# Linear attention and a gated layer on one core: where the output projection accumulates, and when the bonus, state and r steps are issued

## The chip, the cores and the metric

The kernel runs on one NeuronCore of a Trainium2 chip. The metric is device time in microseconds (us) of one execution. Before the change three runs gave 119.29, 119.60 and 119.94 us, median 119.6.

## What is computed

Batch 4, 8 heads, 768 steps, head size 48, so 384 columns for each step. The first half is a recurrence with a 48x48 state for each head, the second a causal convolution over five steps that gates a projection:

```python
for t in range(S):
    cur = np.einsum('bhd,bhe->bhde', u[None] * kt, vt)
    y[:, :, t] = np.einsum('bhd,bhde->bhe', rt, state + cur)
    state = w[None, :, :, None] * state + np.einsum('bhd,bhe->bhde', kt, vt)
...
gate_pre += conv_w[k][None, None, :] * xp[:, k:k + S, :]   # k = 0..4
gate = 1.0 / (1.0 + np.exp(-gate_pre))
val = x @ w_val
return (gate * val @ w_out)
```

## The kernel before

The recurrence is computed in chunks of 128 steps. Two chunks make a unit of 256 steps, so a batch has 3 units and there are N = 12 units. The loop at the end (L551) runs iterations i = 0 to 12, as a software pipeline of two stages: iteration i does the attention side of unit i and the output side of unit f = i - 1. Nothing reorders the instructions afterwards: each engine executes them as the loop writes them, and semaphore waits are put in where tiles depend on each other.

Steps of an iteration, in the order in which TensorE (PE) gets them:

- `y_out(f)` (L390): 80 small matmuls in two PSUM banks, one for each chunk. ScalarE (ACT) copies each bank to `xT` (L428).
- `attn(i)` (L324): scores of the two chunks, each in its own two-bank tile `at_ps` of a pool with two such tiles. VectorE (DVE) multiplies each with the causal mask (`mask_at`, L343).
- `conv(f)` (L431): 40 matmuls, then two sigmoids on ACT (`gate`, L453).
- `bonus(i)` (L298): 8 tiny matmuls into columns 384 to 399 of the one `kv_ps` bank; DVE copies them out to `s_sb` (L314), which stands on DVE behind the two masks. GpSimd (POOL) multiplies v with it (`dv`, L317).
- `transp_r` (L243): transposes of one head pair of a later batch's r, which POOL (in the start-up DVE) has scaled into a ring of four buffers `rs` (L236). They go to the single `tr_ps` bank and are copied to `rT` (L250).
- `value(f)` (L456): x times w_val into two PSUM banks; DVE multiplies each with its gate into `hT` (L480).
- `state(i, 0)` (L350), into columns 0 to 383 of the same `kv_ps` bank that held the bonus, and on DVE `decay` (L379), which writes `z` (L385).
- `transp_k(i+1)` (L270) into `tr_ps`; ACT copies it to `kT` (L280); DVE makes `pr` of it (L291).
- `project(f)` (L485): for each of the two chunks three matmuls with 384 columns, into a bank of the pool `ps_mm`, and an ACT copy to `o_sb` (L499). The pool `ps_mm` has two banks, which `y_out`, `conv`, `value` and `project` take in turn.
- `state(i, 1)`, which the last unit of a batch lacks, and in some iterations a second `transp_r`.

The table `r_plan` (L539) says in which iterations the head pairs of batches 1, 2 and 3 are scaled and transposed. SyncE (SP) issues all loads in program order, k and v three iterations ahead. The weight w_out is loaded by three DMAs (L195 to L197), 768 KB, since the last of the three row tiles is kept a second time with its halves exchanged; one ACT cast makes `wout` of it (L229).

Of the kernel before, what the change touches and what calls it, by code (L numbers as in the profile page):

```python
# [8 lines left out]
F32 = mybir.dt.float32  # L9
# [7 lines left out]
def kernel(  # L17
# [169 lines left out]


    wv_st = consts.tile([128, NT, DM], F32)
    wo_st = consts.tile([128, 4, DM], F32)  # L190

    def load_weights():
        nc.sync.dma_start(out=wv_st, in_=moe_w_val.rearrange("(t p) n -> p t n", p=128))
        wo = moe_w_out.rearrange("(t p) n -> p t n", p=128)
        nc.sync.dma_start(out=wo_st[:, 0::2, :], in_=wo[:, 0::2, :])  # L195
        nc.sync.dma_start(out=wo_st[64:128, 1::2, :], in_=wo[0:64, 1:3, :])
        nc.sync.dma_start(out=wo_st[0:64, 1::2, :], in_=wo[64:128, 1:3, :])  # L197

    wval = consts.tile([128, NT, 4, 128], BF16)
    wout = consts.tile([128, 4, DM], BF16)  # L200
# [23 lines left out]
    def cast_weights():  # L224
        wv = wv_st.rearrange("p k (t x) -> p k t x", x=128)
        nc.gpsimd.tensor_copy(wval[:, :, 0::2, :], wv[:, :, 0::2, :])
        nc.gpsimd.tensor_copy(wval[:, :, 1::2, 64:128], wv[:, :, 1:3, 0:64])
        nc.gpsimd.tensor_copy(wval[:, :, 1::2, 0:64], wv[:, :, 1:3, 64:128])
        nc.scalar.copy(out=wout, in_=wo_st)  # L229


    st = {}
# [1 line left out]
    def scale_r(b, p, eng):  # L234
        hs = slice(2 * p, 2 * p + 2)
        eng.tensor_tensor(  # L236
            out=rs_t[p][:, :, :, 0:D].rearrange("p j a d -> p a j d"),
            in0=r_st[b][:, hs, :].rearrange("p a (j d) -> p a j d", d=D),
            in1=dr[:, hs],
            op=ALU.mult,  # L240
        )

    def transp_r(b, p, dve=False, pool=None):  # L243
        if p == 0:
            st["rT", b] = wk.tile([128, NP, S], BF16, name="rT", bufs=3)
        pool, name = (ps_mm, "mm_ps") if pool else (ps_tr, "tr_ps")
        tr = pool.tile([128, J, 128], BF16, name=name)
        for j in range(J):
            nc.tensor.transpose(tr[:, j, :], rs_t[p][:, j].rearrange("p a x -> p (a x)"), ident)  # L249
        (nc.vector.tensor_copy if dve else nc.scalar.copy)(  # L250
            out=st["rT", b][:, p, :].rearrange("x (p j) -> x p j", j=J),
            in_=tr.rearrange("x j p -> x p j"),
        )
# [231 lines left out]
    def project(n):  # L485
        b, cu = divmod(n, NU)
        hT = st["hT", n]
        o_sb = outp.tile([128, U, DM], F32, name="o_sb")
        for cl in range(U):
            o_ps = ps_mm.tile([128, DM], F32, name="mm_ps")  # L490
            for j, (i, c0) in enumerate(((0, cl * C), (1, cl * C), (cl, W))):
                nc.tensor.matmul(  # L492
                    out=o_ps,
                    lhsT=hT[:, i, c0 : c0 + C],
                    rhs=wout[:, 2 + cl if j == 2 else i, :],
                    start=(j == 0),
                    stop=(j == 2),
                )
            nc.scalar.copy(out=o_sb[:, cl, :], in_=o_ps)  # L499
# [11 lines left out]
    def ok(n):  # L511
        return 0 <= n < N

    load_weights()
    load_kv(1, "v")
    load_kv(2, "k")
    prep_conv()
    spin(80)
# [11 lines left out]
    for par in range(2):  # L530
# [5 lines left out]
        nc.gpsimd.tensor_copy(wcm[rows, :, par, :], wct[rows, :, None].to_broadcast([64, NP, D]))  # L536


    r_plan = {  # L539
        1: (1, (0, 1)),  # L540
        2: (1, (2, 3)),
        3: (2, (0, 1)),
        4: (2, (2,)),
        5: (2, (3,)),
        6: (3, (0, 1)),
        7: (3, (2,)),
        8: (3, (3,)),
    }
    r_load = {0: 1, 2: 2, 4: 3}

    for i in range(N + 1):  # L551
        f = i - 1
        if i == 0:
            load_kv(2, "v")
        if i in r_load:
            load_r(r_load[i])
        if ok(i + 3):
            load_kv(i + 3, "kv")
        rb, rp = r_plan.get(i, (0, ()))
        if ok(f):  # L560
            y_out(f)
        if ok(i + 1):
            cast_v(i + 1)
        for p in rp[:1]:
            scale_r(rb, p, nc.gpsimd)
        if ok(i + 1):
            scale_k(i + 1, nc.gpsimd)
        for p in rp[1:]:
            scale_r(rb, p, nc.gpsimd)
        if ok(i):  # L570
            for cl in range(U):
                attn(i, cl)
                mask_at(i, cl)
        if ok(f):
            conv(f)
        if ok(i):
            bonus(i)
            bonus_v(i)
        if rp:
            transp_r(rb, rp[0])  # L580
# [9 lines left out]
        ends = i % NU == NU - 1  # L590
        for p in rp[1:] if ends else ():
            transp_r(rb, p)
        if ok(i + 1):
# [7 lines left out]
        for p in () if ends else rp[1:]:  # L601
            transp_r(rb, p)
# [1 line left out]
_INS = ['r', 'k', 'v', 'w', 'u', 'moe_w_val', 'moe_conv_w', 'moe_w_out']  # L604
_OUTS = [((4, 768, 384), 'float32')]
# [25 lines left out]
```

## Time and profile before

| | |
|---|---|
| median of three runs | 119.6 us |
| the profiled execution's own time | 118.9 us |
| its span, first to last instruction | 116.4 us |
| mean granted TensorE clock | 0.932 |
| busy share of the span: PE, DVE, ACT, POOL | 82%, 59%, 62%, 55% |
| `y_out` starts of iterations 3, 4, 7, 8, 9 in the trace | 43.19, 50.75, 72.80, 79.59, 86.54 us |

A row of the timeline has the start in us, the duration, the engine, the line, the operation, the tiles, and in brackets how long the engine sat idle before and what ended that. Durations of PE rows contain the latency of the last matmul, so that the next row starts before the row ends. In a row of the waits stand who waited for whom, the sum in us, the number of times and the longest. A row of the windows gives for each engine the busy time in that stretch, then the granted clock (PEclk).

### The profile page before, as it was taken

To read this page: it belongs to the slowest core of one execution; us is meant where nothing else is said; L and a number is where in the kernel's file an instruction comes from. 1 tells how busy PE (TensorE), PEld (TensorE's weight loads), DVE (VectorE), ACT (ScalarE), POOL (GpSimd) and SP (SyncE) were. 2 spreads that over 40 slices of the span, in tenths; PEclk is the share of its full clock that TensorE was granted. 3 is DMA by queue.
4 is the path that set the end of the run, shared out by engine and by line. 5 is a ranking of instruction groups with operands and counts; after the bars stand their busy time and mean duration, and the time that the engine had idled before them with its cause. 6 is when DMAs were issued, how large, how long until landed. Compare 5 with 4: busy or idle time off the path is not lost.

```text
span 116.4 us, 5181 instructions
## 1 busy us (share of the span) xinstructions
PE 95.0 (82%) x2285; PEld 78.4 (67%) x2285; DVE 68.7 (59%) x110; ACT 72.5 (62%) x130; POOL 64.5 (55%) x71
## 2 busy tenths in 40 slices
PE   5999536763989779989979898999988998989660
PEld 5699425553858658769768685887967787785520
DVE  5397594073454925749739297484956779493030
ACT  4396970782268767787656886868768474834430
POOL 7963448207998578781935969469280825013000
PEclk9999965685599999999999999999999999999996
DMA  1999999999899989799979888892873030110303
GB/s 27 298 241 199 260 269 183 203 247 276 172 202 220 340 206 260 161 246 271 299 156 245 179 206 170 219 194 76 187 156 143 0 135 6 68 72 6 141 0 135
DMA packets 58578, 20.60 MB, mean 177 GB/s; under 512 B 50486, under 2 KB 58556, under 8 KB 58556
## 3 DMA queue, kind: packets, MB, share of 16 engines
q1 hardware_dynamic: 58428, 20.26, 71.9%
q8 instruction: 18, 0.29, 1.1%
q0 software_dynamic: 128, 0.00, 0.1%
q14 instruction: 4, 0.03, 0.1%
HBM read 15.54 MB, written 4.72 MB: 174 GB/s over the span
## 4 chain that ended last, share of the span: by engine, by line
PE 56%; SPq 17%; ACT 10%; DMA 5%; issue 4%; DVE 4%; POOL 1%; ACTq 0%; DVEq 0%; POOLq 0%
PE mm_ps L400 12%; SPq L72 12%; PE mm_ps L444 10%; PE mm_ps L463 8%; PE mm_ps L492 5%; PE at_ps L331 5%; DMA r_st<-in_r_dram 5%; PE tr_ps L249 4%; PE tr_ps L277 4%; ACT o_sb L499 4%; ACT kT L280 4%; PE mm_ps L472 3%; DVE pr L291 2%; DVE hT L480 2%; PE kv_ps L305 2%
## 5 line engine op out<-in xcount | busy, mean ns | idle before, releaser
L343 DVE TENSOR_TENSOR at<-at_ps,mask 128x1024 bf16<-128x1024 f32 x24 | 28.2, 1219 | 13.2 <-PE at_ps L331 13.2
L317 POOL TENSOR_TENSOR dv<-v_st,s_sb 128x768 bf16<-128x768 f32 x12 | 17.7, 1475 | 29.4 <-DVE s_sb L314 28.1
L256 POOL TENSOR_TENSOR ks<-k_st,dk 128x768 bf16<-128x768 f32 x11 | 20.0, 1819 | 1.6 <-DMA k_st<-in_k_dram 1.6
L236 POOL TENSOR_TENSOR rs<-r_st,dr 128x576 bf16<-128x576 f32 x12 | 16.8, 1402 | 6.9 <-DMA r_st<-in_r_dram 6.9
L280 ACT COPY kT<-tr_ps 128x1024 bf16<-128x1024 bf16 x11 | 11.1, 1011 | 12.3 <-PE tr_ps L277 12.3
L480 DVE TENSOR_TENSOR hT<-mm_ps,gate 128x384 bf16<-128x384 f32 x24 | 12.7, 557 | 9.7 <-PE mm_ps L472 8.4
L291 DVE TENSOR_TENSOR pr<-tr_ps,rT 128x1024 bf16<-128x1024 bf16 x11 | 7.6, 692 | 13.0 <-ACT kT L280 13.0
L492 PE MATMUL mm_ps<-wout,hT 128*128 128x384 bf16 x72 | 14.4, 327 | 0.5 <-DVE hT L480 0.5
L453 ACT ACTIVATE gate<-mm_ps 128x384 bf16<-128x384 f32 x24 | 10.5, 488 | 6.5 <-PE mm_ps L444 6.4
L428 ACT CAST xT<-mm_ps 128x384 bf16<-128x384 f32 x24 | 11.2, 480 | 4.1 <-PE mm_ps L400 3.4
L463 PE MATMUL mm_ps<-xT,wval 128*128 128x256 bf16 x72 | 12.5, 284 | 1.5 <-ACT gate L453 1.5
L250 ACT COPY rT<-tr_ps 128x768 bf16<-128x768 bf16 x13 | 10.5, 805 | 4.6 <-PE tr_ps L249 4.6
L444 PE MATMUL mm_ps<-xT,cwd 64*64 64x256 bf16 (+1 forms) x480 | 12.5, 247 | 1.0 <-ACT xT L428 0.6
L499 ACT COPY o_sb<-mm_ps 128x384 f32<-128x384 f32 x24 | 10.6, 490 | 4.2 <-PE mm_ps L492 4.2
L265 ACT CAST vb<-v_st 128x768 bf16<-128x768 f32 x12 | 10.0, 835 | 4.6 <-DMA v_st<-in_v_dram 4.6
L444 PEld LDWEIGHTS <-cwd 64*64 64x64 bf16 x480 | 11.5, 107 | 1.9 <-issue 0.5
L385 DVE TENSOR_TENSOR z<-kv_ps,wcm 128x384 bf16<-128x384 f32 x20 | 11.0, 549 | 1.6 <-PE kv_ps L369 0.9
L331 PE MATMUL at_ps<-rT,kT 48*128 48x128 bf16 x192 | 7.6, 217 | 3.4 <-ACT kT L280 2.8
L400 PE MATMUL mm_ps<-at,vb 128*32 128x128 bf16 x384 | 10.2, 226 | 0.1
L492 PEld LDWEIGHTS <-hT 128*128 128x128 bf16 x72 | 6.4, 98 | 4.8 <-DVE hT L480 2.0
L249 PE MATMUL tr_ps<-ident,rs 128*128 128x128 bf16 x78 | 6.8, 225 | 3.4 <-POOL rs L236 1.9
L127 PE MATMUL mm_ps<-ident 128*128 128x128 bf16 x96 | 8.3, 268 | 1.4 <-POOL ident masks.py:199 1.4
(74 smaller groups left out, 156.9 us busy)
## 6 DMA issues: line engine op xcount, KB each, us to landing
k_st<-in_k_dram SPq DMA_DIRECT2D x24, 192.0 KB, 4.7
v_st<-in_v_dram SPq DMA_DIRECT2D x24, 192.0 KB, 4.0
out_dram<-o_sb SPq DMA_DIRECT2D x11, 384.0 KB, 3.4
r_st<-in_r_dram SPq DMA_DIRECT2D x6, 576.0 KB, 5.5
r_st<-in_r_dram SPq DMA_DIRECT2D x4, 288.0 KB, 4.0
wv_st<-in_moe_w_val_dram SPq DMA_DIRECT2D x1, 576.0 KB, 5.1
wo_st<-in_moe_w_out_dram SPq DMA_DIRECT2D x1, 384.0 KB, 6.2
wo_st<-in_moe_w_out_dram SPq DMA_DIRECT2D x2, 192.0 KB, 5.5
```

Source lines behind the costliest of these rows:

```text
L72: nc.sync.dma_start(out=d[n][:, cl], in_=src[b, :, t0 : t0 + C, :].transpose([1, 0, 2]))
L236: eng.tensor_tensor(out=rs_t[p][:, :, :, 0:D].rearrange("p j a d -> p a j d"), in0=r_st[b][:, hs, :].rearrange("p a (j d) -> p a j d", d=D ...
L256: eng.tensor_tensor(out=ks_t[n % 3][:, :, :, :, 0:D].rearrange("p c n a d -> p c (n a) d"), in0=k_st[n], in1=dk[:, None, :, :].to_broadcas ...
L280: nc.scalar.copy(out=st["kT", n].rearrange("x n (c i) -> x c n i", c=U), in_=tr)
L317: nc.gpsimd.tensor_tensor(out=dv_t[n % 2].rearrange("p c (h d) -> p (c h) d", d=D), in0=v_st[n].rearrange("p c h d -> p (c h) d"), in1=st[ ...
L343: nc.vector.tensor_tensor(out=st["at", n, cl].rearrange("p a n i -> p (a n) i"), in0=st["at_ps", n, cl].rearrange("p a n i -> p (a n) i"), ...
L400: nc.tensor.matmul(out=y_ps[32 * q : 32 * q + 32, T, :], lhsT=lt, rhs=rh, start=q not in first, stop=last, skip_group_check=True,)
L444: nc.tensor.matmul(out=g_ps[i][64 * qo : 64 * qo + 64, o0 : o0 + n0], lhsT=cwd[rows, T, t, :], rhs=xT[rows, T, t0 + c0 + t : t0 + c0 + t + ...
L463: nc.tensor.matmul(out=v_ps[:, 0:W], lhsT=wval[:, kt, i, :], rhs=xT[:, kt, t0 : t0 + W], start=(kt == 0), stop=(kt == NT - 1), skip_group_ ...
L480: nc.vector.tensor_tensor(out=hT[:, i], in0=v_ps, in1=st["gate", n][:, i], op=ALU.mult)
L492: nc.tensor.matmul(out=o_ps, lhsT=hT[:, i, c0 : c0 + C], rhs=wout[:, 2 + cl if j == 2 else i, :], start=(j == 0), stop=(j == 2),)
L499: nc.scalar.copy(out=o_sb[:, cl, :], in_=o_ps)
```

## The change

Five edits:

1. `project` accumulates in a tile of the score pool `ps_at`, both chunks in one tile of two banks, in place of two banks of `ps_mm`. Its matmuls are put so that the first two of chunk 0 need only the first half of `hT`.
2. `state(i, 0)` is issued directly behind `bonus`, ahead of `transp_r` and `value`. Its `decay` stays behind `value`, except in iteration 0.
3. r of batch 1 (the second batch): nothing of it is transposed in iteration 1 any more. Pairs 0 and 1 are scaled on POOL at the end of iteration 1, pair 2 on POOL and pair 3 on DVE in iteration 2, and all four transposes stand in iteration 2, pairs 1 and 3 copied by DVE; `transp_k(3)` and `prod(3)` come behind them. In the other iterations the second transpose always follows `state(i, 1)`.
4. w_out is loaded once, by one DMA of 576 KB; three ACT casts make `wout` of it. The v of unit 1 is loaded ahead of the weights.
5. v of unit 1 is cast behind the weight casts.

```diff
+    wo_st = consts.tile([128, NT, DM], F32)
...
-        nc.sync.dma_start(out=wo_st[:, 0::2, :], in_=wo[:, 0::2, :])
-        nc.sync.dma_start(out=wo_st[64:128, 1::2, :], in_=wo[0:64, 1:3, :])
-        nc.sync.dma_start(out=wo_st[0:64, 1::2, :], in_=wo[64:128, 1:3, :])
+        nc.sync.dma_start(out=wo_st, in_=moe_w_out.rearrange("(t p) n -> p t n", p=128))
...
-        nc.scalar.copy(out=wout, in_=wo_st)
+        nc.scalar.copy(out=wout[:, 0::2, :], in_=wo_st[:, 0::2, :])
+        nc.scalar.copy(out=wout[64:128, 1::2, :], in_=wo_st[0:64, 1:3, :])
+        nc.scalar.copy(out=wout[0:64, 1::2, :], in_=wo_st[64:128, 1:3, :])
...
+        oo_ps = ps_at.tile([128, 2, NP, 128], F32, name="at_ps")
         for cl in range(U):
-            o_ps = ps_mm.tile([128, DM], F32, name="mm_ps")
-            for j, (i, c0) in enumerate(((0, cl * C), (1, cl * C), (cl, W))):
+            o_ps = oo_ps[:, cl].rearrange("p n x -> p (n x)")[:, 0:DM]
+            parts = [(0, cl * C, 0), (1, cl * C, 1)]
+            parts.insert(1 + cl, (cl, W, 2 + cl))
+            for j, (i, c0, k) in enumerate(parts):
...
-                    rhs=wout[:, 2 + cl if j == 2 else i, :],
+                    rhs=wout[:, k, :],
...
+    load_kv(1, "v")
     load_weights()
-    load_kv(1, "v")
...
-        2: (1, (2, 3)),
+        2: (1, (), (2,), (), (0, 1, 2, 3)),
...
         if ok(i):
             bonus(i)
             bonus_v(i)
-        if rp:
-            transp_r(rb, rp[0])
-        if ok(f):
-            value(f)
-        if ok(i):
             state(i, 0)
-            decay(i, 0)
+        for p in r2:
+            scale_r(rb, p, nc.gpsimd)
+        if i == 2:
+            scale_r(rb, 3, nc.vector)
         if i == 0:
+            decay(0, 0)
             state(0, 1)
             decay(0, 1)
             cast_weights()
...
+            cast_v(1)
+        if rt:
+            transp_r(rb, rt[0])
+        if ok(f):
+            value(f)
+        if ok(i) and i > 0:
+            decay(i, 0)
+        if i == 2:
+            transp_r(rb, 1, dve=True)
+        elif ok(i + 1):
             transp_k(i + 1)
             prod(i + 1)
         if ok(f):
             project(f)
+        if i == 2:
+            transp_r(rb, 2)
         if ok(i) and i > 0:
             state(i, 1)
             decay(i, 1)
+        if i == 2:
+            transp_r(rb, 3, dve=True)
+            transp_k(i + 1)
+            prod(i + 1)
+        else:
+            for p in rt[1:]:
+                transp_r(rb, p)
```

Three places show what the built programs make of it. `Activation_49`, `DVE_49`, `PE_49` and `Pool_49` are the semaphores of ACT, DVE, PE and POOL; the lines of the changed kernel stand some lower or higher than those of the one before.

The first is PE in iteration 9, behind the convolution. Before, the last bonus matmul (L305) is followed by the value matmuls (L463, L472) and these by the state matmuls (L360):

```order
L305 MATMUL kv_ps<-uw_205,pr 128x2
L463 LDWEIGHTS wval
L463 MATMUL mm_ps<-xT_190,wval 128x256 [waits Activation_49]
...
L472 MATMUL mm_ps<-xT_190,wval 128x128
L360 LDWEIGHTS ks_177
L360 MATMUL kv_ps<-vb_185,ks_177 128x96 [waits DVE_49]
```

In the changed kernel (bonus L304, state L359, value L462):

```order
L304 MATMUL kv_ps<-uw_205,pr 128x2
L359 LDWEIGHTS ks_177
L359 MATMUL kv_ps<-vb_185,ks_177 128x96 [waits DVE_49]
...
L462 LDWEIGHTS wval
L462 MATMUL mm_ps<-xT_190,wval 128x256 [waits Activation_49]
```

The state matmuls have moved ahead of the value matmuls with their wait on DVE. The value waited for there is that of the copy to `s_sb`, in both kernels.

The second is PE at the projection of iteration 8 and the start of `y_out` behind it, before (L492, L400):

```order
L492 LDWEIGHTS hT [waits DVE_49]
L492 MATMUL mm_ps<-wout,hT 128x384 [waits PE_49]
L492 LDWEIGHTS hT [waits DVE_49]
...
L492 MATMUL mm_ps<-wout,hT 128x384 [waits PE_49]
L492 LDWEIGHTS hT
...
L400 MATMUL mm_ps<-rT,z 32x128 [waits Activation_49]
```

And in the changed kernel (L494, L399), where the second wait for `hT` stands before the third matmul:

```order
L494 LDWEIGHTS hT [waits DVE_49]
L494 MATMUL at_ps<-wout,hT 128x384
L494 LDWEIGHTS hT [waits DVE_49]
...
L494 MATMUL at_ps<-wout,hT 128x384 [waits Activation_49]
L494 LDWEIGHTS hT
...
L399 MATMUL mm_ps<-rT,z 32x128 [waits PE_49]
```

The wait for ACT has moved from the first matmul of `y_out` to the fourth matmul of the projection, the first of chunk 1. The value waited for is that of the first copy to `o_sb` of the same projection: both chunks write one tile now. On ACT that copy stands behind the copy to `kT`, as before.

The third is PE at the end of iteration 2 in the changed kernel, where r of batch 1 is transposed (L248) around the projection and ahead of `transp_k` (L276):

```order
L248 MATMUL tr_ps<-ident,rs_181 128x128 [waits Activation_49]
...
L494 LDWEIGHTS hT [waits DVE_49]
...
L248 MATMUL tr_ps<-ident,rs_182 128x128 [waits DVE_49]
...
L248 MATMUL tr_ps<-ident,rs_183 128x128 [waits Activation_49]
...
L276 MATMUL tr_ps<-ident,ks_177 128x128 [waits DVE_49]
```

Each of the four waits for the copy of the step before it out of the one `tr_ps` bank, by ACT and DVE in turn. Before, one such transpose stood at the end of iteration 1 and two in iteration 2, of which only the last stood directly ahead of `transp_k`.

More of the change, by code (lines that the diff above doesn't have):

```diff
@@ L189 @@
     wv_st = consts.tile([128, NT, DM], F32)
-    wo_st = consts.tile([128, 4, DM], F32)
+    wo_st = consts.tile([128, NT, DM], F32)
     def load_weights():
         nc.sync.dma_start(out=wv_st, in_=moe_w_val.rearrange("(t p) n -> p t n", p=128))
-        wo = moe_w_out.rearrange("(t p) n -> p t n", p=128)
-        nc.sync.dma_start(out=wo_st[:, 0::2, :], in_=wo[:, 0::2, :])
-        nc.sync.dma_start(out=wo_st[64:128, 1::2, :], in_=wo[0:64, 1:3, :])
-        nc.sync.dma_start(out=wo_st[0:64, 1::2, :], in_=wo[64:128, 1:3, :])
+        nc.sync.dma_start(out=wo_st, in_=moe_w_out.rearrange("(t p) n -> p t n", p=128))
     wval = consts.tile([128, NT, 4, 128], BF16)
@@ L539 @@
     r_plan = {
-        1: (1, (0, 1)),
-        2: (1, (2, 3)),
[L542 to L547, printed above, removed]
+        1: (1, (), (), (0, 1), ()),
+        2: (1, (), (2,), (), (0, 1, 2, 3)),
+        3: (2, (0,), (1,), (), (0, 1)),
+        4: (2, (2,), (), (), (2,)),
+        5: (2, (3,), (), (), (3,)),
+        6: (3, (0,), (1,), (), (0, 1)),
+        7: (3, (2,), (), (), (2,)),
+        8: (3, (3,), (), (), (3,)),
     }
@@ L558 @@
             load_kv(i + 3, "kv")
-        rb, rp = r_plan.get(i, (0, ()))
+        rb, r0, r1, r2, rt = r_plan.get(i, (0, (), (), (), ()))
         if ok(f):
             y_out(f)
-        if ok(i + 1):
+        if ok(i + 1) and i > 0:
             cast_v(i + 1)
-        for p in rp[:1]:
+        for p in r0:
             scale_r(rb, p, nc.gpsimd)
@@ L567 @@
             scale_k(i + 1, nc.gpsimd)
-        for p in rp[1:]:
+        for p in r1:
             scale_r(rb, p, nc.gpsimd)
@@ L589 @@
             cast_weights()
[L590 to L593, printed above, removed]
+            cast_v(1)
[8 more added lines that the diff above has]
+        elif ok(i + 1):
             transp_k(i + 1)
@@ L600 @@
             decay(i, 1)
-        for p in () if ends else rp[1:]:
-            transp_r(rb, p)
+        if i == 2:
[5 more added lines that the diff above has]
+                transp_r(rb, p)
 _INS = ['r', 'k', 'v', 'w', 'u', 'moe_w_val', 'moe_conv_w', 'moe_w_out']
```

## Prediction

> **What bounds the kernel now.** I read the page first, then who waited for whom, then the timeline of single iterations, and last the granted clock by windows.
>
> ```profile
> span 116.4 us, 5181 instructions
> PE 95.0 (82%) x2285; PEld 78.4 (67%) x2285; DVE 68.7 (59%) x110; ACT 72.5 (62%) x130; POOL 64.5 (55%) x71
> ```
>
> PE is the fullest engine, and what counts is when it stands still. The waits:
>
> ```profile
> PE mm_ps L400 <- ACT o_sb L499: 2.4, 6, 0.6
> PE kv_ps L360 <- DVE s_sb L314: 2.0, 1, 2.0
> PE tr_ps L249 <- POOL rs L236: 1.9, 1, 1.9
> PE mm_ps L463 <- ACT gate L453: 1.5, 4, 0.6
> ```
>
> The first, third and fourth are what this change touches: `y_out` waiting for the output copies, r of batch 1 arriving late, `value` waiting for the gates. The second tells most. In iteration 0, the only one in which the state matmuls follow the bonus at once, they waited 2.0 us for the copy to `s_sb` and started 0.06 us after its end:
>
> ```profile
> 17.67 0.16 DVE L314 COPY s_sb<-kv_ps 128x16 f32<-128x16 f32 x1
> 17.89 0.50 PE L360 MATMUL kv_ps<-vb,ks 128*128 128x96 bf16 x4 [1.97 <-DVE s_sb L314]
> ```
>
> Iteration 8 shows where that copy stands otherwise:
>
> ```profile
> 81.27 2.35 DVE L343 TENSOR_TENSOR at<-at_ps,mask 128x1024 bf16<-128x1024 f32 x2 [0.92 <-PE at_ps L331]
> 82.42 0.35 PE L305 MATMUL kv_ps<-uw,pr 128*128 128x2 bf16 x8
> 82.64 0.49 PE L249 MATMUL tr_ps<-ident,rs 128*128 128x128 bf16 x6
> 83.54 0.16 DVE L314 COPY s_sb<-kv_ps 128x16 f32<-128x16 f32 x1
> 84.39 0.61 PE L277 MATMUL tr_ps<-ident,ks 128*128 128x128 bf16 x8
> 84.84 1.14 PE L492 MATMUL mm_ps<-wout,hT 128*128 128x384 bf16 x6
> 85.09 1.01 ACT L280 COPY kT<-tr_ps 128x1024 bf16<-128x1024 bf16 x1 [1.00 <-PE tr_ps L277]
> 86.00 0.87 ACT L499 COPY o_sb<-mm_ps 128x384 f32<-128x384 f32 x2
> 86.54 0.35 PE L400 MATMUL mm_ps<-rT,z 128*32 128x128 bf16 x12 [0.56 <-ACT o_sb L499]
> ```
>
> DVE spends 81.27 to 83.54 on the two masks, so `s_sb` ends at 83.70, while PE is through with the bonus at 82.64. PE fills that gap with transposes and `value`. Likewise the first output copy on ACT starts at 86.00, behind `kT`, long after its three matmuls; PE has used that time for the second three.
>
> **The state matmuls behind the bonus.** PE takes its instructions in order, and behind the state matmuls stand `transp_r`, `value`, `transp_k` and the projection. The state can start 0.06 us after `s_sb`, here at 83.76. PE then idles from 82.64 to 83.76, 1.12 us, where it idled nowhere. The work moved does not change in length. Iterations 3 to 7 differ from this by 0.1 at most: six times 1.12, 6.7 us. In iterations 9 to 11 there is no r left, and part of the wait was there already:
>
> ```profile
> 89.37 0.35 PE L305 MATMUL kv_ps<-uw,pr 128*128 128x2 bf16 x8
> 90.02 0.49 PE L463 MATMUL mm_ps<-xT,wval 128*128 128x256 bf16 x3 [0.29 <-ACT gate L453]
> 90.48 0.17 DVE L314 COPY s_sb<-kv_ps 128x16 f32<-128x16 f32 x1
> ```
>
> The first instruction behind the bonus starts at 90.02 now, and would start at 90.71 (90.48 + 0.17 + 0.06): 0.69 us more, in 9 and in 10. In 11 the state's 0.33 us lay beside the wait for `hT`; ahead of `value` it lies on the path, so 1.0. That is 2.4, and 9.1 us in all. The bounds are 0.1 us either way for each of the nine.
>
> **The projection in the score banks.** The wait of `y_out` for the copies goes. But the fourth matmul now waits for the first copy, and that copy is queued behind `kT`. From the start of `transp_k` at 84.39 the first copy ends at 86.49 and releases PE at 86.54: 2.15 us. What started at that moment was `y_out`; now it is the second three matmuls, 0.50 us (half of 0.99), and `y_out` comes behind them. So 0.5 us are added, not saved. Where `state(i, 1)` follows, it stood in the shadow of the wait and no longer does; iteration 7:
>
> ```profile
> 77.45 0.61 PE L277 MATMUL tr_ps<-ident,ks 128*128 128x128 bf16 x8
> 78.87 0.33 PE L360 MATMUL kv_ps<-vb,ks 128*128 128x96 bf16 x4
> 79.59 0.35 PE L400 MATMUL mm_ps<-rT,z 128*32 128x128 bf16 x12 [0.23 <-ACT o_sb L499]
> ```
>
> Again 2.14 from `transp_k` to `y_out`; now 2.15 + 0.50 + 0.33 = 2.98, so 0.83 more, in 4, 7, 9 and 10: 3.3 us. In 3 and 6 a transpose follows that waited for `pr` anyway, so 0.5 there as in 5 and 8: 2.0 us. The last two projections have no `kT` ahead of them; the last of all:
>
> ```profile
> 110.01 0.49 PE L463 MATMUL mm_ps<-xT,wval 128*128 128x256 bf16 x3 [0.58 <-ACT gate L453]
> 110.77 1.05 DVE L480 TENSOR_TENSOR hT<-mm_ps,gate 128x384 bf16<-128x384 f32 x2 [4.90 <-PE mm_ps L472]
> 112.42 0.96 ACT L499 COPY o_sb<-mm_ps 128x384 f32<-128x384 f32 x2 [2.08 <-PE mm_ps L492]
> ```
>
> The new order runs one matmul more before the second half of `hT`: 0.16 us gained. Then the first copy must end (0.54 from its start), three matmuls run (0.33 to the start of the third and 0.38 from there to the copy), and the second copy starts at 1.25 where it started at 0.48 (half of 0.96). Net 0.6 us in 12; in 11, where `y_out` follows, 0.50 - 0.16 = 0.35. Together 6.3 us.
>
> **Weights, v and r at the start.** Iteration 1:
>
> ```profile
> 27.00 0.16 DVE L314 COPY s_sb<-kv_ps 128x16 f32<-128x16 f32 x1
> 28.36 0.82 PE L249 MATMUL tr_ps<-ident,rs 128*128 128x128 bf16 x6 [1.90 <-POOL rs L236]
> 28.97 0.85 PE L463 MATMUL mm_ps<-xT,wval 128*128 128x256 bf16 x3
> 31.53 1.02 PE L277 MATMUL tr_ps<-ident,ks 128*128 128x128 bf16 x8
> 34.86 0.35 PE L400 MATMUL mm_ps<-rT,z 128*32 128x128 bf16 x12
> ```
>
> The clock stood at half from 28.98 to 32.39:
>
> ```profile
> 28.98:32.39 3.41, 3.41 (x28) 2.87 (x27) 1.67 (x3) 0.80 (x1) 3.41 (x3) 0.50 0.91 177
> ```
>
> Without r the state starts at 27.22, behind `s_sb`; state and value take 2.56 (28.97 to 31.53). `transp_k` would start at 29.8 at half clock, or 29.4 if the clock is up by 29. From there 2.98 to `y_out` at full clock gives 32.4, not 34.86: a gain of 2.4 us; if the clock stays low until 32.4, 33.4, a gain of 1.5. I take 2.4, since PE then stands still little after 27.2. That w_out is loaded once saves 192 KB of loads ahead of r; its three casts on ACT stand ahead of `kT` of unit 1 and take up to 0.8 us longer than the one did. I set both at nothing against each other, with 0.7 us either way.
>
> In iteration 2 the four transposes come together:
>
> ```profile
> L250 ACT COPY rT<-tr_ps 128x768 bf16<-128x768 bf16 x13 | 10.5, 805 | 4.6 <-PE tr_ps L249 4.6
> L250 DVE COPY rT<-mm_ps 128x768 bf16<-128x768 bf16 x1 | 1.0, 957 | 0.7 <-PE mm_ps L249 0.7
> 38.80 0.16 DVE L314 COPY s_sb<-kv_ps 128x16 f32<-128x16 f32 x1
> 43.19 0.35 PE L400 MATMUL mm_ps<-rT,z 128*32 128x128 bf16 x12 [0.56 <-ACT o_sb L499]
> ```
>
> From `y_out` (34.86) the state starts at 4.16 (38.80 + 0.22); state, first transpose and value take 1.75 as in iteration 8 (82.64 to 84.39), so 5.91; the second transposes end at 6.34. Their copy on DVE stands behind `hT` and `z` and ends at about 8.2, the projection as well. Third transposes to 8.65; ACT, busy with the second output copy until 8.85, copies to 9.65; fourth from 9.7, copied on DVE from 10.2 to 11.2; `transp_k` to 11.7, and `y_out`. It took 8.33 (34.86 to 43.19): 3.4 us more. At least 2.4, if the copies start a quarter of a microsecond earlier each.
>
> **The clock.** Cut into stretches of 3.41 us, the granted clock is whole or half in each:
>
> ```profile
> 11.93:15.34 3.41, 1.88 (x35) 1.40 (x32) 1.82 (x3) 3.41 (x5) 1.81 (x3) 1.00 0.98 289
> 15.34:18.75 3.41, 0.98 (x16) 0.66 (x13) 2.75 (x5) 1.45 (x2) 1.50 (x2) 0.50 1.15 212
> 107.50:110.91 3.41, 2.25 (x75) 2.03 (x64) 0.14 (x1) 1.64 (x4) 0.00 (x0) 1.00 0.33 120
> 110.91:114.33 3.42, 1.57 (x10) 0.57 (x8) 0.91 (x2) 0.96 (x2) 0.00 (x0) 1.00 0.16 58
> ```
>
> The first column is PE's busy time. After 1.88 the clock fell to half for the next stretch, after 2.25 it did not. At the end of iteration 2 PE idles 2.6 us out of 4.2, so a stretch there falls to about 1.8 or less for most positions, and the next runs at half clock: `transp_k` and `y_out` take longer, up to 1.7 us; I take 1.0, between that and nothing. The Trainium skill, in "TensorE: Matmul & The Clock Gate", section "Why this matters for your kernels", asks only that PE not idle for more than about 3 us; no gap here is that long, so by it this term would be nothing and the time 1.0 us less. The first stretch speaks against it: PE idled 1.53 us in it altogether.
>
> **The sum.** 9.1 + 6.3 - 2.4 + 3.4 + 1.0 = 17.4 us. The profiled execution took 118.9 us (span 116.4 and 2.5 around it) and would take 136.3; the median of the runs lies 0.7 higher, so I forecast 137.0 us.
>
> **Rivals.**
>
> *The clock also falls in the later iterations* (0.13). Each has two gaps of about 1 us. A stretch of 3.41 us holds at most one of them whole, so PE is busy in 2.3 us of it, just above the 2.25 that kept the clock. For it: the margin is thin. Against: no stretch so full lost the clock. If one stretch in three fell, at some 1.1 us each, 4 us come on top: 141; if one in each iteration, 10: 147. The Trainium skill, same page, section "A second HAM failure mode: psum-queue depth-cycling", tells of short idles between matmul groups, from cycling through PSUM banks, that made the clock swing. That would be this case; no run here shows it so far.
>
> *Only the state's wait is paid* (0.05), the projection's second half being ready in time. Then the 6.3 and the 2.4 us of `y_out`'s waits go: about 128. Against: the copy stands behind `kT` in every iteration up to 10.
>
> *Faster* (0.02). If the masks ended before the bonus, and the first output copy before the third matmul, the waits for copies (2.4), the gate waits of 0.29 in 9 to 11 and iteration 1 (2.4) would be won, against 2 us in iteration 2: 116. It decides at masks of 1.37 us for both (81.27 to 82.64); they take 2.27.
>
> **Numbers.** The forecast has 0.79, no measurable change 0.01. Its range: the nine state waits and ten projections 0.1 each way (1.9), iteration 1 up to 0.9 worse, iteration 2 up to 1.0 better, the clock -1.0 to +0.7, the loads 0.7 either way; added, 132.4 to 141.2; taking off what would all have to come together below, 133 to 141. It takes in the mild case of the clock rival. A run can tell 0.5% from no change: faster 0.02, same 0.01, slower 0.97.
>
> **What would show it.** In the profile after: PE waiting for `s_sb` about 1 us in each of iterations 3 to 11, and for `o_sb` at the projection instead of at `y_out`; `y_out` starts 7.8 to 9.2 us apart; no wait for `rs` in iteration 1; half clock after iteration 2. It is wrong if the state starts within 0.3 us of the bonus, if the fourth projection matmul follows the third at once, or if half clock comes back after 50 us.

## The result, and the profile after

The changed kernel took 136.58 us, the median of four runs (134.75 to 137.67), beside 119.77 us for the kernel before (119.29 to 120.0, four runs). Ratio after to before: 1.1304, 95% interval 1.12 to 1.1409. The change makes the kernel some 13% slower; 137.0 us had been forecast. The ratios, here and below, leave out executions that were disturbed (the two slowest of the changed kernel, of which 137.67 us is the profiled one; in kernel C below among others two of 135.66 and 176.14 us), so that prices are read from the profiles and the ratios rather than from the medians alone.

The head of the page after, with busy time per engine, and the granted clock in 40 slices of 3.39 us:

```profile
span 135.5 us, 5174 instructions
PE 98.8 (73%) x2285; PEld 78.6 (58%) x2285; DVE 72.2 (53%) x113; ACT 73.7 (54%) x130; POOL 63.6 (47%) x70
PEclk9999968658999689999999999999999999999997
```

TensorE runs the same 2285 matmuls. It is busy 3.8 us longer; 2.4 of that is the projection (16.8 us against 14.4), whose two halves now run apart, so that each row contains the latency of a last matmul. But the span grew by 19.1: for 15.3 us of it TensorE stands still. The waits (total, count, longest) say for what:

```profile
PE kv_ps L359 <- DVE s_sb L313: 11.9, 12, 2.0
PE at_ps L494 <- ACT o_sb L501: 10.5, 12, 1.0
PE at_ps L330 <- ACT kT L279: 4.2, 2, 3.1
PE tr_ps L276 <- DVE rT L249: 1.0, 1, 1.0
```

The first was 2.0 us in one iteration and is 11.9 in all twelve. The second is new, once per iteration; `y_out`'s wait for `o_sb` (2.4) and the transposes' for `rs` (1.9) are gone. Here is iteration 8 (by the lines of the changed kernel: `bonus` L304, `state` L359, projection L494, `y_out` L399):

```profile
93.45 2.36 DVE L342 TENSOR_TENSOR at<-at_ps,mask 128x1024 bf16<-128x1024 f32 x2 [1.01 <-PE at_ps L330]
94.61 0.35 PE L304 MATMUL kv_ps<-uw,pr 128*128 128x2 bf16 x8
95.72 0.17 DVE L313 COPY s_sb<-kv_ps 128x16 f32<-128x16 f32 x1
95.94 0.33 PE L359 MATMUL kv_ps<-vb,ks 128*128 128x96 bf16 x4 [0.97 <-DVE s_sb L313]
...
97.65 0.61 PE L276 MATMUL tr_ps<-ident,ks 128*128 128x128 bf16 x8
98.35 1.01 ACT L279 COPY kT<-tr_ps 128x1024 bf16<-128x1024 bf16 x1 [0.75 <-PE tr_ps L276]
98.09 0.72 PE L494 MATMUL at_ps<-wout,hT 128*128 128x384 bf16 x3
99.26 0.48 ACT L501 COPY o_sb<-at_ps 128x384 f32<-128x384 f32 x1
99.79 0.65 PE L494 MATMUL at_ps<-wout,hT 128*128 128x384 bf16 x3 [0.98 <-ACT o_sb L501]
100.37 0.35 PE L399 MATMUL mm_ps<-rT,z 128*32 128x128 bf16 x12
```

Both mechanisms are in these ten rows. VectorE is in the two masks until 95.72, while TensorE has been through with the bonus since 94.96 (94.61 + 0.35); the copy to `s_sb` follows the masks and the state follows the copy, 0.97 us late. Then three matmuls of the projection run, but ScalarE is in `kT` and copies the first half of the output only from 99.26 to 99.74, and 0.05 us after that the other three matmuls start, 0.98 us late.

Against the kernel before, by the starts of `y_out`, the 19.1 us of span divide like this:

| stretch | before | after | difference | forecast |
|---|---|---|---|---|
| start to `attn` of iteration 1 | 24.15 | 25.03 | +0.9 | 0 |
| from there to `y_out` of iteration 2 | 10.71 | 9.32 | -1.4 | -2.4 (bound -1.5) |
| to `y_out` of iteration 3 | 8.33 | 12.01 | +3.7 | +3.4 |
| to `y_out` of iteration 4 | 7.56 | 10.19 | +2.6 | 1.12 + 0.5 + 1.0 = 2.6 |
| to the end of the span | 65.65 | 78.95 | +13.3 | 9.1 + 6.3 - 1.12 - 0.5 = 13.8 |

### The profile page after: what moved, and what is told of

Same layout as the page of the kernel before. It is cut to its first block, busy times and chain, and to the rows that moved or that the text cites. A ratio compares the mean times of both kernels' runs of the same rounds, so it can differ in the third digit from the quotient of the medians.

```text
span 135.5 us, 5174 instructions
## 1 busy us (share of the span) xinstructions
PE 98.8 (73%) x2285; PEld 78.6 (58%) x2285; DVE 72.2 (53%) x113; ACT 73.7 (54%) x130; POOL 63.6 (47%) x70
## 4 chain that ended last, share of the span: by engine, by line
PE 42%; issue 17%; SPq 12%; ACT 11%; DVE 8%; DMA 7%; ACTq 0%; DVEq 0%
PE mm_ps L399 9%; SPq L72 9%; PE at_ps L494 8%; PE mm_ps L462 5%; ACT o_sb L501 5%; DMA wo_st<-in_moe_w_out_dram 5%; DVE at L342 5%; PE tr_ps L276 4%; PE kv_ps L359 3%; PE at_ps L330 3%; PE mm_ps L471 3%; PE tr_ps L248 3%; DMA v_st<-in_v_dram 2%; ACT kT L279 2%; PE mm_ps L443 2%
## 5 line engine op out<-in xcount | busy, mean ns | idle before, releaser
L316 POOL TENSOR_TENSOR dv<-v_st,s_sb 128x768 bf16<-128x768 f32 x12 | 18.2, 1513 | 52.1 <-DVE s_sb L313 52.1
L494 PE MATMUL at_ps<-wout,hT 128*128 128x384 bf16 x72 | 16.8, 327 | 10.9 <-ACT o_sb L501 10.5
L501 ACT COPY o_sb<-at_ps 128x384 f32<-128x384 f32 x24 | 11.5, 481 | 14.9 <-PE at_ps L494 14.9
L494 PEld LDWEIGHTS <-hT 128*128 128x128 bf16 x72 | 5.5, 97 | 18.4 <-issue 13.2
L359 PE MATMUL kv_ps<-vb,ks 128*128 128x96 bf16 x80 | 6.9, 211 | 12.7 <-DVE s_sb L313 11.9
L235 POOL TENSOR_TENSOR rs<-r_st,dr 128x576 bf16<-128x576 f32 x11 | 15.4, 1405 | 0.8 <-DMA r_st<-in_r_dram 0.8
L452 ACT ACTIVATE gate<-mm_ps 128x384 bf16<-128x384 f32 x24 | 10.5, 488 | 7.1 <-PE mm_ps L443 7.1
L359 PEld LDWEIGHTS <-ks 128*128 128x128 bf16 x80 | 5.6, 99 | 14.5 <-issue 11.5
L443 PE MATMUL mm_ps<-xT,cwd 64*64 64x256 bf16 (+1 forms) x480 | 13.2, 254 | 0.9 <-ACT xT L427 0.6
L249 ACT COPY rT<-tr_ps 128x768 bf16<-128x768 bf16 x11 | 8.8, 801 | 8.5 <-PE tr_ps L248 8.5
L443 PEld LDWEIGHTS <-cwd 64*64 64x64 bf16 x480 | 12.0, 111 | 2.1 <-issue 0.8
L462 PE MATMUL mm_ps<-xT,wval 128*128 128x256 bf16 x72 | 12.5, 284 | 0.6 <-ACT gate L452 0.6
L399 PE MATMUL mm_ps<-at,vb 128*32 128x128 bf16 x384 | 10.4, 232 | 0.0
```

The costliest lines, as they stand in the source:

```text
L235: eng.tensor_tensor(out=rs_t[p][:, :, :, 0:D].rearrange("p j a d -> p a j d"), in0=r_st[b][:, hs, :].rearrange("p a (j d) -> p a j d", d=D ...
L316: nc.gpsimd.tensor_tensor(out=dv_t[n % 2].rearrange("p c (h d) -> p (c h) d", d=D), in0=v_st[n].rearrange("p c h d -> p (c h) d"), in1=st[ ...
L359: nc.tensor.matmul(out=kv_ps[:, p], lhsT=ks[:, cl, p].rearrange("p a x -> p (a x)"), rhs=heads(vb[:, cl], H)[:, 2 * p : 2 * p + 2, :], sta ...
L399: nc.tensor.matmul(out=y_ps[32 * q : 32 * q + 32, T, :], lhsT=lt, rhs=rh, start=q not in first, stop=last, skip_group_check=True,)
L443: nc.tensor.matmul(out=g_ps[i][64 * qo : 64 * qo + 64, o0 : o0 + n0], lhsT=cwd[rows, T, t, :], rhs=xT[rows, T, t0 + c0 + t : t0 + c0 + t + ...
L462: nc.tensor.matmul(out=v_ps[:, 0:W], lhsT=wval[:, kt, i, :], rhs=xT[:, kt, t0 : t0 + W], start=(kt == 0), stop=(kt == NT - 1), skip_group_ ...
```

## The experiments

In each kernel below, `attn(n)` is the start of the score matmuls of iteration n in its profiled run. The stretch from attn(1) to attn(4) holds what the change does to r and to the clock, with three iterations of the two waits; the stretch from attn(4) to the end of the span holds the waits alone, in nine iterations. The kernel before is run beside each; its medians were 119.77 (with the change), 119.26, 119.11 and 119.01 us in the four sets.

| kernel | median us | ratio to before, 95% | attn(1) to attn(4) | attn(4) to end |
|---|---|---|---|---|
| before | | 1 | 27.66 | 64.6 |
| the change | 136.58 | 1.1304 (1.12 to 1.1409) | 32.59 | 77.9 |
| A: state back | 126.08 | 1.0615 (1.0538 to 1.0693) | 29.66 | 70.2 |
| B: projection back | 128.30 | 1.0794 (1.0682 to 1.0907) | 29.57 | 71.4 |
| C: both back | 118.30 | 0.9907 (0.9844 to 0.9969) | 26.90 | 64.9 |
| D: bonus between the masks | 126.00 | 1.0593 (1.0518 to 1.0669) | 29.72 | 70.2 |
| E: two score tiles | 125.64 | 1.0556 (1.0487 to 1.0626) | 29.92 | 69.3 |
| F: D and E | 115.97 | 0.9668 (0.9589 to 0.9746) | 26.63 | 62.6 |
| G: F, old r | 115.29 | 0.9664 (0.9601 to 0.9726) | 24.79 | 64.0 |
| H: G, old loads | 115.70 | 0.9705 (0.9642 to 0.9768) | 27.26 | 62.6 |
| I: before, projection in two score tiles | 115.57 | 0.9744 (0.9681 to 0.9807) | 27.44 | 61.7 |
| J: the change, old r | 134.44 | 1.1333 (1.1253 to 1.1412) | 29.77 | 78.0 |
| K: the change, old loads | 136.13 | 1.1501 (1.1426 to 1.1576) | 31.85 | 77.8 |
| L: before, state early, bonus between the masks | 118.47 | 0.9987 (0.9937 to 1.0036) | 27.58 | 65.1 |

**A: the state matmuls go back behind `value`.** All else of the change stays.

```diff
             bonus_v(i)
-            state(i, 0)
...
         if ok(i) and i > 0:
+            state(i, 0)
             decay(i, 0)
```

> The changed kernel with one edit undone: state(i, 0) stands behind the value matmuls again. If its wait for s_sb costs what the sum says (about 1.1 us in iterations 3 to 8, 0.7 to 1.0 in 9 to 11), the time falls by 9.1 us against the changed kernel's 136.6, to 127.5, and the waits of the state matmuls for s_sb after iteration 0 are gone. If the loss were made by the regrouped r and the weights at the start, or by the clock, it would stay above 134.

Measured 126.08 us. The wait for `s_sb` is back to its one case in iteration 0, that for `o_sb` stays:

```profile
PE at_ps L494 <- ACT o_sb L501: 11.1, 12, 1.0
PE kv_ps L359 <- DVE s_sb L313: 2.0, 1, 2.0
```

The last nine iterations give 77.9 - 70.2 = 7.7 us, where the forecast had 9.1 - 1.12 = 8.0 for them; over the whole kernel it is 10.5 us by the medians and 0.069 of 119.3, 8.2 us, by the ratios (9.1 were expected).

**B: the projection goes back to the other pool** (`mm_ps` for each chunk), the state stays early.

```diff
-        oo_ps = ps_at.tile([128, 2, NP, 128], F32, name="at_ps")
         for cl in range(U):
-            o_ps = oo_ps[:, cl].rearrange("p n x -> p (n x)")[:, 0:DM]
+            o_ps = ps_mm.tile([128, DM], F32, name="mm_ps")
```

> The changed kernel with the projection back in the two banks of ps_mm, its new order of matmuls kept. If the wait of the second three matmuls for the first output copy costs 0.5 to 0.8 us in each iteration, the time falls by 6.3 us to 130.3, and PE waits for o_sb at y_out again, 2 to 3 us in all. If the start or the clock made the loss, it stays above 134.

Measured 128.30 us. Now the wait at the projection is gone and a smaller one at `y_out` is back (1.3 us, where 2 to 3 were expected):

```profile
PE kv_ps L359 <- DVE s_sb L313: 11.9, 12, 2.0
PE mm_ps L399 <- ACT o_sb L500: 1.3, 4, 0.5
```

In the last nine iterations 77.9 - 71.4 = 6.5 us, against 6.3 - 0.5 = 5.8 forecast; over the whole 8.3 us by the medians, 6.1 by the ratios.

**C: both back** (the edits of A and B together).

> Both edits undone; what is left of the change is the r of batch 1, the weights and the order of the projection's matmuls. If the two waits are independent and make up nearly all, 15.4 us go and 121.2 us are left, 1 to 2 us above the kernel before. If the two waits overlap (one filling the other's gap), it would be the single undoings that give less than their sum: e1 and e2 together less than 13 us.

Measured 118.30 us: the last nine iterations are again those of before (64.9 and 64.6), so the two moves are all that costs there, and their prices nearly add: 77.9 - 64.9 = 13.0, against 7.7 + 6.5 = 14.2. (Each is worth 1.2 us less once the other is gone: 71.4 - 64.9 = 6.5 for the state, 70.2 - 64.9 = 5.3 for the projection.) The expectation had the whole at 121.2 and missed: without the two waits what is left of the change is a gain of 0.9% (0.3 to 1.6), not a loss of 2 us. Of the 2.0 us that the forecast's terms for iterations 1, 2 and the clock came to, the waits of iterations 1 and 2 are a part.

**D: the state stays early, but the bonus is issued between the two masks,** and with it the copy to `s_sb`.

```diff
-            for cl in range(U):
-                attn(i, cl)
-                mask_at(i, cl)
+            attn(i, 0)
+            mask_at(i, 0)
+            attn(i, 1)
+            bonus(i)
+            mask_at(i, 1)
+            bonus_v(i)
```

(The two calls of the bonus behind `conv` are gone.)

> The state matmuls stay where the change put them, but the bonus and its copy to s_sb are issued between the two score chunks' masks, so that the copy stands behind one mask on DVE and not two. If the place of the copy in DVE's queue is what the state waits for, the waits go as in e1 and the state fills the gap ahead of the gates in iterations 9 to 11 as well: 9.1 + 0.9 = 10 us less, 126.6. If it is the sharing of the bank by bonus and state itself, whatever the queue, the time stays at 136.

Measured 126.00 us, as much as taking the early state away. So it isn't the place of the state that costs, but that its copy is queued behind both masks. (The bonus also moves ahead of the convolution, which then fills the time until the copy is done.) F, which has the same edit, shows the order in one iteration:

```profile
92.15 1.23 DVE L342 TENSOR_TENSOR at<-at_ps,mask 128x1024 bf16<-128x1024 f32 x1 [0.57 <-PE at_ps L330]
92.26 0.35 PE L304 MATMUL kv_ps<-uw,pr 128*128 128x2 bf16 x8
92.55 1.02 PE L443 MATMUL mm_ps<-xT,cwd 64*64 64x256 bf16 x40
93.29 0.17 DVE L313 COPY s_sb<-kv_ps 128x16 f32<-128x16 f32 x1
93.38 1.22 DVE L342 TENSOR_TENSOR at<-at_ps,mask 128x1024 bf16<-128x1024 f32 x1
93.51 0.33 PE L359 MATMUL kv_ps<-vb,ks 128*128 128x96 bf16 x4
```

The copy stands between the masks, ends while TensorE is in the convolution, and the state starts without a wait.

**E: the change, with a score tile of its own for each chunk of the projection.**

```diff
-        oo_ps = ps_at.tile([128, 2, NP, 128], F32, name="at_ps")
         for cl in range(U):
-            o_ps = oo_ps[:, cl].rearrange("p n x -> p (n x)")[:, 0:DM]
+            oo_ps = ps_at.tile([128, 2, NP, 128], F32, name="at_ps")
+            o_ps = oo_ps[:, 0].rearrange("p n x -> p (n x)")[:, 0:DM]
```

> The change with one thing altered: each chunk of the projection has a score tile of its own, instead of both sharing one. The theory that the sharing of one tile makes the fourth matmul wait for the first output copy expects PE's wait for o_sb at the projection (10.5 us over 12) to go but for a few tenths, and, since the second copy no longer holds y_out either (y_out's products go to another pool), a gain of at least the 8.3 us that moving the projection back gave: 127 to 128.5 us, the wait for s_sb still 11.9 us. The rival, that the score tile is late because attn's mask reads it and not because of the copy, expects the wait to stay at 0.5 us or more per iteration under another releaser (DVE at) and 132 us or more.

Measured 125.64 us. The end of its iteration 8, where TensorE doesn't stop between the halves:

```profile
90.27 0.61 PE L276 MATMUL tr_ps<-ident,ks 128*128 128x128 bf16 x8
90.71 1.21 PE L494 MATMUL at_ps<-wout,hT 128*128 128x384 bf16 x6
90.97 1.01 ACT L279 COPY kT<-tr_ps 128x1024 bf16<-128x1024 bf16 x1 [0.75 <-PE tr_ps L276]
91.85 0.35 PE L399 MATMUL mm_ps<-rT,z 128*32 128x128 bf16 x12
91.88 0.87 ACT L501 COPY o_sb<-at_ps 128x384 f32<-128x384 f32 x2
```

All six matmuls run at once and `y_out` starts 0.03 us before the first copy: neither the halves nor `y_out` wait, and E's list of waits has no `o_sb` left (`s_sb` has 11.4 us). That is faster than the 127 to 128.5 us expected. `kT` still stands ahead of that copy; it costs nothing any more. So the wait came from the two halves sharing one tile, not from the score banks. It is worth 77.9 - 69.3 = 8.6 us in the last nine iterations, 2.1 more than B, where `y_out` waits for the copies again (1.3 us in its listed waits).

**F: the edits of D and E together, all of the change kept.**

> The change with both waits taken away and all its edits kept: the bonus and its copy issued between the two masks, so that the state matmuls behind it find s_sb ready, and a score tile for each chunk of the projection. If the two waits are the whole loss and add up (undoing the one alone gave 10.5 us, the other alone 8.3), 136.6 - 10.5 - 8.3 = 117.8 us, and up to 2.4 us less if the waits of y_out for o_sb that stood in the kernel before (2.4 us over 6) are gone as well: 115.5 to 118. If work behind the waits (ACT's copies) becomes the bound when they go, 120 or more.

Measured 115.97 us, 3.3% faster than the kernel before (2.5 to 4.1). With the two waits taken away and nothing undone, the loss is gone: the theory needs no third cause. What binds then is seen in two stretches of 20 us (the second number is TensorE's busy time):

```profile
60.00:80.00 20.00, 19.47 (x530) 15.78 (x530) 14.37 (x22) 15.60 (x28) 15.21 (x10) 1.00 0.92 210
80.00:100.00 20.00, 19.56 (x560) 15.39 (x548) 15.18 (x25) 12.88 (x24) 7.96 (x5) 1.00 0.38 105
```

TensorE is busy 97 to 98% of the time, against 18.69 and 18.54 us in the same stretches before.

**G and H: F with r scaled and transposed as before; H with the loads, casts and v as before too.**

```diff
-        1: (1, (), (), (0, 1), ()),
-        2: (1, (), (2,), (), (0, 1, 2, 3)),
+        1: (1, (0,), (1,), (), (0, 1)),
+        2: (1, (2,), (3,), (), (2, 3)),
```

(and the special cases for `i == 2` go; for H `load_weights` and `cast_weights` of before.)

> As the run with both waits taken away, but r of batch two scaled and transposed in iterations 1 and 2 as in the kernel before. The prediction had r's regrouping at -2.4 us in iteration 1 and +3.4 in iteration 2. If iteration 1 gains only the 0.5 us seen and iteration 2 loses 3.4 of which the two waits were about 1.6, the old plan is worth 1 to 1.5 us against the run beside it. If the regrouping is a gain by itself once the waits are gone (the run with both moves undone was 1 us faster than the kernel before), this run is 1 to 2 us slower than the one beside it.

> As the run before it (both waits taken away, r as in the kernel before), and with the weights and v of unit 1 loaded and cast as in the kernel before too. The three casts of w_out took 2.5 us ahead of kT of unit 1 where the one took 1.5, so about 1 us faster than the run before it if the casts are on the path of iteration 1, no difference within 0.5 us if the earlier load makes up for them.

Measured 115.29 and 115.70 us: no difference from F or from each other that these runs can tell, so the expectations of 1 us or more missed; of H's two, that of no difference within 0.5 us held. The profiles show why less remains than expected. In H's list of waits the transposes of r stand still for r of batch one in iteration 1, as in the kernel before:

```profile
PE tr_ps L249 <- POOL rs L236: 1.9, 1, 1.9
```

In G's list, with the smaller loads ahead of r, almost not:

```profile
PE tr_ps L248 <- POOL rs L235: 0.2, 1, 0.2
```

So from attn(1) to attn(4) G is 2.5 us quicker than H (24.79 against 27.26), but 1.4 us slower from there on. G's timeline has two stops of TensorE there for which the profile shows no releaser:

```profile
57.42 0.57 PE L330 MATMUL at_ps<-rT,kT 48*128 48x128 bf16 x14 [1.29 <-issue]
67.31 0.33 PE L471 MATMUL mm_ps<-xT,wval 128*128 128x128 bf16 x3 [0.68 <-issue]
```

They come to 2.0 us. The first is not G's alone: in the same place, behind the first two score matmuls of iteration 5, F stops for 0.59 us, H for 0.78 and the kernel before for 0.68. Why they stop, and whether G's other runs do, isn't known.

**I: the kernel before with the projection alone moved, in two score tiles.**

```diff
+            oo_ps = ps_at.tile([128, 2, NP, 128], F32, name="at_ps")
-            o_ps = ps_mm.tile([128, DM], F32, name="mm_ps")
+            o_ps = oo_ps[:, 0].rearrange("p n x -> p (n x)")[:, 0:DM]
```

(with the change's order of the three matmuls.)

> The kernel before with the projection alone moved to the score banks, each chunk in a tile of its own (state matmuls, r and loads as before). What the move can save is the wait of y_out for o_sb (2.4 us over 6) and the 0.16 us of one matmul run ahead of the second half of hT. Theory: with no shared tile nothing is added, so 119.1 - 2.4 = 116.7 us, 116 to 118. Rival, that the score banks hold up attn or the copies: no gain, 118.5 or more.

Measured 115.57 us, ratio 0.9744 (0.9681 to 0.9807): 3.0 us faster, a little more than the 2.4 of `y_out`'s waits, and by the median just under the 116 to 118 expected. Most of the gain that F has over the kernel before is this one move.

**J: the change with r as before. K: the change with loads, casts and v as before.** J has G's edit of the table and of the cases for `i == 2` on the unaltered change; K has

```diff
-        nc.scalar.copy(out=wout[:, 0::2, :], in_=wo_st[:, 0::2, :])
-        nc.scalar.copy(out=wout[64:128, 1::2, :], in_=wo_st[0:64, 1:3, :])
-        nc.scalar.copy(out=wout[0:64, 1::2, :], in_=wo_st[64:128, 1:3, :])
+        nc.scalar.copy(out=wout, in_=wo_st)
...
-    load_kv(1, "v")
     load_weights()
+    load_kv(1, "v")
```

and the three loads of `w_out` and the place of the cast of v of unit 1 as before.

> The change with r of batch one and two scaled and transposed as in the kernel before; both waits stay. The prediction's terms for r were -2.4 us in iteration 1, +3.4 in iteration 2 and +1.0 for the clock after it, so by them undoing it gives 136.6 - 2.0 = 134.6 us. What the profile showed, -0.5 in iteration 1 and 3.7 in iteration 2 of which about 1.6 belongs to the two waits, with the clock, gives 134 to 136. The runs with both waits taken away showed no difference between the two plans of r (115.97 and 115.29 us), by which it would stay at 136 to 137.

> The change with w_out loaded and cast as in the kernel before (in four slots, one cast) and v of unit 1 loaded and cast as before; all else kept. The prediction set these edits at nothing, 0.7 us either way: 135.9 to 137.3 us. If the three casts ahead of kT (2.5 us against 1.5) are on the path, 135.6 (1 us faster); the runs with both waits away, 115.29 and 115.7 us, speak for no difference.

J took 134.44 us, 2.1 less than the change by the medians, where the forecast's terms give 2.0; by the ratios (intervals 1.1253 to 1.1412 and 1.12 to 1.1409) the two can't be told apart. The profile places it: from attn(1) to attn(4) J takes 29.77 us, the change 32.59, K 31.85, and from attn(4) on all three are alike (78.0, 77.9, 77.8). So r's regrouping costs 2.8 us in these two profiled runs, all of it ahead of attn(4) (1.8 between F and G). K took 136.13 us: by the median the weights and v make no difference that shows (0.7 either way was forecast). By the ratios K is the slower one, with intervals (1.1426 to 1.1576 and 1.12 to 1.1409) that don't meet, so the new loads may be worth a little; but the two ratios come from different sets. J and K ran in one set and differ beyond their intervals too, but in r and in the loads at once, so that pair doesn't say which of the two it is.

**L: the kernel before with the state matmuls alone moved, and the bonus between the masks** (the projection in its old banks, but with the change's order of its matmuls).

```diff
+            attn(i, 1)
+            bonus(i)
+            mask_at(i, 1)
+            bonus_v(i)
...
+            state(i, 0)
...
-            state(i, 0)
```

> The kernel before with the state matmuls alone moved behind the bonus, and the bonus with its copy issued between the two masks (projection in its old banks, r and loads as before). If the state's wait is only that for s_sb behind both masks, this move costs nothing: 118.5 to 119.5 us, or down to 118 where waits for the gate (1.5 us over 4) now lie beside the state matmuls. With s_sb behind both masks it would be 9 us more, 128.

Measured 118.47 us, ratio 0.9987 (0.9937 to 1.0036): the early state is free if `s_sb` is there, and gains nothing.

## Why the prediction was right

**The state behind the bonus: right.** Forecast 9.1 us in iterations 3 to 11. The trace has one wait of 0.97 us (1.03 in iteration 3) in each of the nine, the copy standing behind both masks. In the nine iterations from attn(4) on, A and D both put its price at 7.7 (6.5 with the projection's wait gone as well), forecast 8.0. The step had 1.12 for an idle of 0.97 because it counted from the start of the next instruction, which overlapped the end of the bonus; in length of an iteration the sizes hold: iteration 8 grew from 6.95 to 8.59 us, by 1.64, and 1.12 + 0.5 were forecast.

**The projection: right.** Forecast 6.3 us, with the fourth matmul waiting for a copy queued behind `kT`; waits of 0.92 to 0.98 us in iterations 3 to 10 and of 0.57 in 11 and 12 show it, B measures 6.5 (5.3 with the state's wait gone as well) where 5.8 was forecast, and E shows the cause to be the shared tile.

**Iteration 1: the mis-sized term.** 2.4 us of gain were forecast and 1.4 came, 0.1 under the bound of 1.5. The step took the clock to be up by 29 us, and for its bound to be low until 32.4. The changed kernel shows, in stretches of 3.41 us (PE busy time first, granted clock third from the end),

```profile
21.43:24.84 3.41, 0.50 (x32) 0.33 (x20) 0.00 (x0) 3.36 (x5) 1.81 (x1) 0.99 0.98 220
24.84:28.25 3.41, 3.09 (x64) 2.52 (x65) 3.12 (x4) 2.03 (x6) 0.00 (x0) 0.51 1.13 327
28.25:31.66 3.41, 3.27 (x25) 2.70 (x25) 1.09 (x3) 0.48 (x2) 3.25 (x3) 0.50 1.03 197
31.66:35.07 3.41, 2.36 (x66) 1.61 (x68) 1.82 (x4) 1.87 (x3) 3.41 (x3) 0.99 0.90 177
```

the clock at half from 24.84 to 31.66, so scores, convolution, state and value of iteration 1 all ran slow, and most of the transposes of k with them. It was at half for just as long in the kernel before, but began 1.4 us behind the start of `attn`, not ahead of it. The step read the second of the two slow stretches and left out the first:

```profile
25.57:28.98 3.41, 1.51 (x39) 1.26 (x31) 1.59 (x3) 1.41 (x3) 2.08 (x2) 0.50 1.00 276
```

From the start of `attn` the state began after 3.36 us, where 27.22 - 24.15 = 3.07 were forecast; `transp_k` 2.51 us later (29.4 - 27.22 = 2.18), and `y_out` 3.45 us after that (2.98). Together this is the missing 1 us. The two new waits, 0.27 for `s_sb` and 1.05 for `o_sb`, are no part of it: the forecast has them in 27.22 and in 2.98. And `attn` of iteration 1 itself started 0.9 later than before. The three casts of `w_out`, which stand ahead of `kT`, look like the reason in this one profile, but the nine kernels with the new loads start it at 24.06 to 25.03, and the kernels with the old ones at 23.83 to 25.08: that looks like scatter, and K, with the old loads and casts, isn't faster beyond it.

**Iteration 2: right.** 3.4 forecast, 3.7 in the profile, with the transposes waiting 0.93 and 1.05 us for the copies of r. J and G, with r as before, take 9.97 and 7.65 us from `y_out` to `y_out` there where the change takes 12.01.

**The clock: right, and its rival fell.** The stretches around the end of iteration 2 and the one after:

```profile
41.89:45.30 3.41, 1.48 (x15) 1.04 (x15) 1.33 (x2) 1.20 (x3) 3.41 (x3) 1.00 0.77 149
45.30:48.71 3.41, 3.29 (x92) 2.89 (x93) 0.76 (x2) 1.49 (x2) 0.52 (x1) 0.51 1.14 281
48.71:52.12 3.41, 2.38 (x75) 2.12 (x76) 2.44 (x3) 2.08 (x4) 0.48 (x1) 0.99 0.49 98
```

PE was busy 1.48 us of 3.41 with no stop above 1.05, and the next stretch ran at half. How little is too little isn't a fixed number: the changed kernel has 1.88 us from 11.20 to 14.61, as much as the row of before that the prediction shows, and kept the full clock in the stretch behind it. Every later stretch to 113.5 us holds 2.38 us or more and keeps the full clock, so two stops of 1 us in each iteration don't cost clock, and 141 to 147 us didn't come. That the Trainium skill ("TensorE: Matmul & The Clock Gate", "Why this matters for your kernels") speaks of idle beyond some 3 us only is not borne out by the first of these rows; the clock swings from short idles that the same page describes under "A second HAM failure mode: psum-queue depth-cycling" don't appear after 50 us.

**The other rivals.** That only the state's wait is paid (128 us) fell with the second wait. The case of a gain, 116 us, had two conditions: the masks out of the bonus's way, and the projection's halves not waiting. F makes both true, by other means than faster copies, and takes 115.97. That the two numbers agree is partly chance: F's profile wins 1.0 us from attn(1) to attn(4) and 2.0 from there on, where that case had 2.4 won in iteration 1, 2 lost in iteration 2 and 3.3 won in waits.

**The sum.** 17.4 us were forecast; the profiled run is 18.8 longer than that of before (137.67 against 118.9), the medians are 16.8 apart, and the ratio's 13.04% of 119.77 is 15.6. Against the table of stretches the start cost 0.9 more, iteration 1 won 1.0 less, iteration 2 cost 0.3 more and the rest 0.5 less. The mechanisms held; that the median lies within 0.5 us of 137.0 is partly luck, since the profiled execution lies 1.4 above its forecast of 136.3.

## What to carry to other kernels

A matmul moved to where its engine is free still starts behind the copy that releases its bank or tile: look up what is queued ahead of that copy on the copying engine, here two masks of 1.2 us and a `kT` of 1.0. Two results that share one tile made the second wait for the first's reader here; a tile for each turned a loss of some 6 us (B against the change) into a gain of 3 (I). When a change loses, look for the order that removes its wait before undoing it: moving a copy of 0.17 us ahead of a mask was worth as much as taking the whole move back.

## What the runs showed that was not expected

The fall of the clock after iteration 2 is not a property of the program's order alone. Kernel E has the same transposes of r, waiting 0.89 and 1.05 us in the same place, and its clock doesn't fall there (slices of 3.09 us):

```profile
PEclk9999985955899999999999999999999999999999
```

The half clock ends here with the eleventh slice. In the change, A, C, D and K the clock falls once more after iteration 2; in B, E and F, which have the same transposes there, it doesn't. Cut at each kernel's own stretches of 3.41 us, the one ahead of the fall has TensorE busy for 1.44 to 1.48 us in those five; in B, E and F the emptiest stretch there has 2.05, 1.90 and 2.03. So in these eight profiles it is where the idle lies against the stretches that separates them, though no run moves the stretches alone. The forecast's "most positions" was right in five of eight, so that the 1.0 us came is partly luck. It may also be why executions of the change differ: the shortest, 134.75 us, has a mean granted clock of 0.957 where the other three have 0.943 or 0.944, and one stretch at half clock less would be 1.3% of its span of 132.5 us (an estimate: half of 3.41 us over 132.5).

The change's loads of the weights and of v removed by themselves the wait for `rs` in iteration 1 (1.9 us in H, 0.2 in G, none in J); the regrouping of r isn't needed for that. It didn't show in the medians of kernels that were already free of the two waits: F, G, H and I lie within 0.7 us. The 2.5 us that G has over H up to attn(4) are seen in one profiled run of each.
